# Retention attention and a noisy top-2 router on one core: a later place for the weight casts of four experts in the order model, and new priority offsets for the expert tiles

## The chip, the core and the metric

The kernel runs on one core of a Trainium2 chip, in one launch. The metric is the device time of one execution in microseconds (us). Each time given is the median of several executions, with the lowest and the highest beside it. The engines are PE (TensorE), DVE (VectorE), ACT (ScalarE), POOL (GpSimd) and SP (SyncE, which only issues transfers here); PEld is PE's loading of weights.

## The reference

The inputs are q, k and v of 8 batches, 8 heads, 576 positions and 64 channels, gate weights, noise, and two weight matrices for each of 8 experts (512 to 1024, and 1024 to 512).

```
scores = (1/8) * q @ k^T                               # per batch and head
Dmat   = gamma_h ** (i - j) where i >= j, else 0       # gamma_h = 1 - 2**(-5-h)
x      = ((scores * Dmat) @ v) as [4608 tokens, 512]   # heads side by side
logits = x @ w_gate + log1p(exp(x @ w_noise)) * noise
top2, weights = the 2 largest of 8 logits, softmax of the two
out[token] = sum over its 2 experts e: weight * (relu(x @ w1[e]) @ w2[e])
```

There is no softmax in the attention, so it is computed in chunks with carried states. Each token goes through two of the eight experts only.

## The kernel before

**How the work is staged.** The attention is done in 16 units of four heads of one batch. Four units and a `tail` (the last 64 positions) make one batch pair, and after each of the four pairs comes `route`: logits on PE (L967), the choice of two experts in some twenty small DVE operations (L977 to L1012, ending with the one-hot matrix MM at L1003), ranks by a triangular matmul on PE (L1030, L1032), a product on POOL (L1041), table positions on DVE, and then two large one-hot products on DVE: `olo` and `oh` (both L1074) and `oh` times values (L1076). PE multiplies these (L1081) into a table `xi` of the tokens of each expert (L1092 to L1099). PE also turns the attention's result into rows (L1110), which SP stores to a buffer `xd` in DRAM.

In one unit, POOL or DVE scales q and v (L721, L728), PE transposes k and q (L744, L750), ACT copies the transposes (L459), PE computes scores (L775), DVE masks them (L783, four per unit), PE makes the states (L808, copied by ACT) and the result (L843, L853). The `tail` has its own lines: products on POOL (L881, L884), transposes (L893), scores (L908), masks on DVE (L913), results (L926, L930).

**The experts.** Each expert has a fixed number of places for tokens, in tiles of 128 rows. Tiles whose tokens are known early run in gaps of the attention: 11 early tiles of one or two row blocks, i = 0 to 10, in the order of experts 0, 0, 1, 1, 2, 2, 0, 1, 2, 3, 3. POOL gathers the rows of a tile by indirect DMA (L1246, tiles `xg`), PE transposes them (L1268), ACT or DVE copies (L459, L461; the latter is DVE's form of the same copy), PE runs the first layer (`up`, L1328), ACT or DVE the relu (L1337, L1339), PE the second layer (`down`, L1418), ACT or DVE the weighting (L1471, L1473), and POOL scatters the rows to the output (L1483). After them come the `wide` tiles of up to four row blocks (first layer L1354, transposed by DMA), the second layer of each tile interleaved with the first of the next.

**The weights.** Experts 0 to 2 are loaded by casting DMAs that POOL issues (L1159, L1163). Expert 3 takes the place of the attention's `xT`, and experts 4 to 7 take the places of 0 to 3: for these, `part` lets SP load eight pieces in f32 (L1183, L1186) to `big` tiles, and ACT or DVE casts each to bf16 (L1188).

**What sets the order.** Nothing is reordered on the chip: each engine runs its own stream in order. The streams are written by a list scheduler, `Plan.run`. `Kernel.record` first enters all operations, each with a model cost, its reads and writes, a buffer class and a priority `prio`. `run` then again and again takes the ready operation with the smallest (earliest model start in steps of 0.05 us, `prio`, number of entry). An operation with two allowed engines goes to the one where the model ends it sooner. The earliest start takes in when an operand is there; for an operand that a DMA brings, `hold` us of the operation are added.

`Plan.op` adds to the given `prio` an offset from the table ORDER, by the name `at` of the operation and a bucket of the given `prio`: buckets 0 to 3 for 0 to 59, bucket 4 for 60 to 135, bucket 5 from 136 up. The attention and the routing lie in 0 to 3. An early tile i is entered at 100 + 4i: tiles 0 to 8, and the casts of expert 3 (60), lie in bucket 4, tiles 9 and 10 and all wide tiles in bucket 5. Offsets of one step of `prio` decide only between operations that the model could start at the same time. Two fillers follow from the model too: `warm` puts matmuls without use (L467) where the model sees PE idle in the first 170 us, and `rest` (L444) puts a memset between indirect DMAs.

Of the kernel before, what the change touches and what calls it, by code (L numbers as in the profile page):

```python
# [21 lines left out]
F = 1024  # L22
# [134 lines left out]
    "route48": (-0.5, -0.25, -1.5, 0, -0.5, -0.5),  # L157
    "route49": (2, 5, 0.5, -1.5, 2, 2),
    "route50": (-2.5, -2, -2, -6.5, -2.5, -2.5),
    "overflow_table1": (-2, -2, -2, -2, -2, -2),  # L160
    "overflow_table2": (-2, -2, -2, -2, -2, -2),
    "overflow_table3": (-0.25, -0.25, -0.25, -0.25, -0.25, -0.25),
    "overflow_table4": (-2, -2, -2, -2, -2, -2),
    "weights1": (-0.75, -0.75, -0.75, -0.75, -0.75, -0.75),
    "part1": (2, 2, 2, 2, 2, 2),
    "fetch1": (-5, -5, -5, -5, -6, -4),
    "fetch2": (-1.25, -1.25, -1.25, -1.25, -1.5, -2.25),
    "fetch3": (0.5, 0.5, 0.5, 0.5, -3, 1.5),
    "fetch4": (-0.25, -0.25, -0.25, -0.25, 0.75, 0.75),
    "fetch5": (0, 0, 0, 0, 0, -4),  # L170
    "fetch6": (-4, -4, -4, -4, -8.25, -1.5),
    "fetch7": (-1.25, -1.25, -1.25, -1.25, 6.5, -3.25),
    "fetch8": (-2.5, -2.5, -2.5, -2.5, -4, 0),
    "mix1": (0.25, 0.25, 0.25, 0.25, 0.25, 0.25),
    "mix2": (4, 4, 4, 4, 4, 4),
    "mix3": (2.25, 2.25, 2.25, 2.25, 2.25, 2.25),
    "up1": (2, 2, 2, 2, 2, 2),
    "wide1": (2.75, 2.75, 2.75, 2.75, 2.75, 2.75),
    "wide2": (1.25, 1.25, 1.25, 1.25, 1.25, 1.25),
    "finish1": (-2.25, -2.25, -2.25, -2.25, -2.25, -2.25),  # L180
    "finish2": (0, 0, 0, 0, 0, 5.5),
    "finish3": (5.75, 5.75, 5.75, 5.75, 24, 6.75),
    "finish4": (5.5, 5.5, 5.5, 5.5, 5.5, 5.5),
    "record1": (3, 3, 3, 3, 3, 3),
    "record2": (1.75, 1.75, 1.75, 1.75, 1.75, 1.75),
    "record3": (6.5, 6.5, 6.5, 6.5, 6.5, 6.5),
    "record4": (2, 2, 2, 2, 2, 2),
}
BIG = 1.0e6
NOV = NCOL * E  # L190
# [223 lines left out]
class Kernel:  # L414
    def __init__(self, tc, ctx, src, gates, noise, w1, w2, out, xd):
# [761 lines left out]
    def part(self, e, k, prio, after):  # L1177
        pl, nc = self.pl, self.nc
        w, t = self.W[e], pl.buf("big", "exp")

        def ld(_):
            if k < KD:
                nc.sync.dma_start(out=t.t, in_=self.w1[e, k * P:(k + 1) * P, :])  # L1183
            else:
                fo = 2 * (k - KD)
                nc.sync.dma_start(out=t.t.rearrange("p (fo d) -> p fo d", fo=2),  # L1186
                                  in_=self.w2[e, fo * P:(fo + 2) * P, :].rearrange("(fo fi) d -> fi fo d", fi=P))
        pl.op("SP", 0.55, ld, w=[t], prio=prio, dma=1.35, after=after)  # L1188
        pl.op({"ACT": 1.06, "DVE": 0.7}, 0, lambda g: self.copy(g, w.t[:, k * F:(k + 1) * F], t.t), hold=1,
              r=[t], w=[(w, k)], prio=prio, at="part1")  # L1190

    def tiles(self):
# [183 lines left out]
    def down(self, i, t):  # L1376
# [372 lines left out]
```

## Time and profile before

| | |
|---|---|
| median of 3 executions | 411.0 us (410.47 to 411.59) |
| profiled execution | 412.69 us |
| its span, first to last instruction | 411.1 us |
| granted PE clock, mean of the span | 0.989 |
| PE busy | 377.1 us, 92% |
| ACT, POOL, DVE busy | 272.3, 291.0, 148.2 us |
| bytes moved by DMA | 98.06 MB, mean 239 GB/s |

The time is that of one execution on the device; the span lies within it. A row of a timeline gives the start and the length of a run of like instructions in us, the engine, line and operation, output and inputs, the count, and in brackets how long the engine had been idle and what ended that ("issue" where the profile shows nothing that was waited for). The ends of matmuls are modelled, so PE's lengths overlap a little; starts are as recorded.

### The profile page before, as it was taken

To read this page: it belongs to the slowest core of one execution; us is meant where nothing else is said; L and a number is where in the kernel's file an instruction comes from. 1 tells how busy PE (TensorE), PEld (TensorE's weight loads), DVE (VectorE), ACT (ScalarE), POOL (GpSimd) and SP (SyncE) were. 2 spreads that over 40 slices of the span, in tenths; PEclk is the share of its full clock that TensorE was granted. 3 is DMA by queue.
4 is the path that set the end of the run, shared out by engine and by line. 5 is a ranking of instruction groups with operands and counts; after the bars stand their busy time and mean duration, and the time that the engine had idled before them with its cause. 6 is when DMAs were issued, how large, how long until landed. Compare 5 with 4: busy or idle time off the path is not lost.

```text
span 411.1 us, 11031 instructions
## 1 busy us (share of the span) xinstructions
PE 377.1 (92%) x4320; PEld 233.3 (57%) x4320; DVE 148.2 (36%) x413; ACT 272.3 (66%) x468; POOL 291.0 (71%) x379
## 2 busy tenths in 40 slices
PE   4998867889898898999999999999999999999994
PEld 2567656677575666767556554544554454454453
DVE  8456798788269587220111322101011000000002
ACT  2589978898787765776555877666686445555451
POOL 8676783990799848778676477778675776728564
PEclk9899999989999999999999999999999999999999
DMA  8999998999999989999989899999999998839766
GB/s 226 290 298 255 317 305 254 306 269 252 275 286 205 264 188 284 395 246 221 280 188 377 288 331 223 260 251 230 296 257 211 165 202 152 164 45 133 127 94 131
DMA packets 106184, 98.06 MB, mean 239 GB/s; under 512 B 40975, under 2 KB 83472, under 8 KB 106130
## 3 DMA queue, kind: packets, MB, share of 16 engines
q1 hardware_dynamic: 85858, 60.92, 56.0%
q0 software_dynamic: 17584, 36.24, 43.4%
q8 instruction: 34, 0.56, 0.6%
q10 hardware_dynamic: 2688, 0.18, 0.4%
q14 instruction: 20, 0.16, 0.2%
HBM read 73.11 MB, written 26.10 MB: 241 GB/s over the span
## 4 chain that ended last, share of the span: by engine, by line
PE 65%; DVE 8%; POOL 7%; DMA 6%; issue 6%; ACT 6%; POOLq 0%; SPq 0%; another core or an unknown queue 0%; DVEq 0%; ACTq 0%
PE ps L1418 25%; PE ps L1354 23%; PE ps L1328 6%; POOL out_dram L1483 4%; DMA xd<-xg 2%; ACT half L459 2%; DMA half<-in_v_dram 2%; DVE half L783 2%; PE ps L1437 2%; PE ps L808 2%; PE ps L467 1%; POOL half L721 1%; ACT xT L459 1%; DVE olo L1074 1%; PE ps L1268 1%
## 5 line engine op out<-in xcount | busy, mean ns | idle before, releaser
L1337 ACT ACTIVATE half<-ps 128x512 bf16<-128x512 f32 (+5 forms) x184 | 90.6, 503 | 87.5 <-PE ps L1354 55.0
L1418 PE MATMUL ps<-W,half 128*128 128x512 bf16 x432 | 137.8, 379 | 1.4 <-issue 1.1
L1354 PE MATMUL ps<-big,W 128*128 128x512 bf16 (+4 forms) x448 | 124.5, 326 | 0.6 <-DVE half L1473 0.6
L1246 POOL DMA_INDIRECT xg<-xd,xi x76 | 79.1, 1040 | 48.2 <-DMA half<-in_v_dram 11.7
L1483 POOL DMA_INDIRECT out_dram<-half,xg x71 | 90.3, 1272 | 30.1 <-issue 14.8
L1418 PEld LDWEIGHTS <-half 128*128 128x128 bf16 x568 | 54.5, 98 | 62.8 <-issue 3.1
L1354 PEld LDWEIGHTS <-W 128*128 128x128 bf16 x448 | 43.8, 98 | 33.4 <-issue 0.8
L1354 PE MATMUL ps<-big,xT 128*128 128x512 bf16 (+2 forms) x160 | 47.6, 337 | 0.0
L1471 ACT ACTIVATE half<-ps,xg 128x512 f32<-128x512 f32 (+1 forms) x58 | 39.3, 678 | 10.0 <-PE ps L1418 6.7
L783 DVE TENSOR_TENSOR half<-ps,mask 128x512 bf16<-128x512 f32 x64 | 40.3, 682 | 14.3 <-PE ps L775 10.9
L1418 PE MATMUL ps<-xT,half 128*128 128x512 bf16 x136 | 44.9, 379 | 0.0
L459 ACT ACTIVATE half<-ps 128x1024 bf16<-128x1024 bf16 (+1 forms) x42 | 38.5, 946 | 7.9 <-PE ps L744 4.0
L1473 DVE TENSOR_SCALAR half<-ps,xg 128x512 f32<-128x512 f32 (+1 forms) x17 | 10.6, 623 | 76.8 <-PE ps L1437 42.0
L1328 PE MATMUL ps<-half,W 128*128 128x256 bf16 (+1 forms) x288 | 29.1, 255 | 1.6 <-DVE half L461 0.8
L1339 DVE TENSOR_SCALAR half<-ps 128x512 bf16<-128x512 f32 (+5 forms) x12 | 6.8, 569 | 60.5 <-issue 32.9
L1328 PEld LDWEIGHTS <-W 128*128 128x128 bf16 x288 | 23.7, 98 | 5.8 <-issue 1.8
L467 PE MATMUL ps<-mask,ident__61 128*128 128x512 bf16 x68 | 20.3, 429 | 3.7 <-DVE hpf L527 3.7
L1469 DVE SCALAR_TENSOR_TENSOR half<-ps,xg,half 64x256 f32<-64x256 f32 (+2 forms) x7 | 3.6, 521 | 55.2 <-PE ps L1437 32.4
L1354 PEld LDWEIGHTS <-xT 128*128 128x128 bf16 x160 | 15.6, 98 | 12.8 <-issue 0.4
L459 ACT ACTIVATE tb<-ps 64x512 bf16<-64x512 f32 x32 | 18.9, 591 | 4.0 <-POOL half L721 1.9
L459 ACT ACTIVATE W<-big 128x1024 bf16<-128x1024 f32 x20 | 21.0, 1059 | 0.0
L808 PE MATMUL ps<-half,half 64*64 64x64 bf16 (+2 forms) x512 | 17.2, 213 | 1.7 <-ACT xT L459 1.6
(204 smaller groups left out, 517.0 us busy)
## 6 DMA issues: line engine op xcount, KB each, us to landing
big<-in_moe_w_dram SPq DMA_DIRECT2D x40, 512.0 KB
W<-in_moe_w_dram POOLq DMA_DIRECT2D x12, 512.0 KB
xd<-xg SPq DMA_DIRECT2D x16, 264.0 KB
W<-in_q_dram SPq DMA_DIRECT2D x16, 256.0 KB
big<-in_k_dram SPq DMA_DIRECT2D x8, 512.0 KB
big<-in_v_dram SPq DMA_DIRECT2D x8, 512.0 KB
big<-in_q_dram SPq DMA_DIRECT2D x16, 256.0 KB
W<-in_k_dram SPq DMA_DIRECT2D x6, 512.0 KB
```

The lines of the kernel that those rows point to most:

```text
L459: self.nc.scalar.activation(out, in_, Act.Copy)
L467: self.nc.tensor.matmul(b.t, lhsT=ident, rhs=mask.rearrange("p r x -> p (r x)").unsqueeze(1).to_broadcast([P, 2, 2 * P]), start=True, stop ...
L783: nc.vector.tensor_tensor(S.t.bitcast(BF16).rearrange("p (h c x) -> p h c x", h=2, c=2)[:, h], p[h].t.rearrange("p (c x) -> p c x", c=2), ...
L808: nc.tensor.matmul(o[h * HD:(h + 1) * HD, hp, n, :], lhsT=kk[:k, r, c, y], rhs=vv[:k, r, c, y].unsqueeze(1).to_broadcast([k, n.stop - n.st ...
L1246: ins = nc.gpsimd.indirect_dma_start(out=x.t[:n, :], out_offset=None, in_=self.xd[:rows, :], in_offset=IOff(ap=xi.t[:n, h:h + 1], axis=0), ...
L1328: nc.tensor.matmul(pv()[:, f2, :], lhsT=w.t[:, o:o + P], rhs=xv()[:, di, :n], start=(di == 0), stop=(di == KD - 1))
L1337: self.nc.scalar.activation(o, i, Act.Relu)
L1354: self.mm = nc.tensor.matmul(p.t[:, :n], lhsT=w.t[:, o:o + P], rhs=xv()[:, di, :n], start=(di == 0), stop=(di == KD - 1))
L1418: self.mm = self.nc.tensor.matmul(po.t, lhsT=hv[:, c:c + P], rhs=self.W[e].t[:, o:o + DM], start=(f == 0), stop=(f == KF - 1))
L1471: nc.scalar.activation(y.t[q, c], x, Act.Copy, scale=g()[q])
L1473: nc.vector.tensor_scalar(y.t[q, c], x, g()[q], None, Alu.mult)
L1483: ins = nc.gpsimd.indirect_dma_start(out=self.out[:, :], out_offset=IOff(ap=ix()[q2], axis=0), in_=y.t[q2, :], in_offset=None, bounds_chec ...
```

## The change

There are two edits. The first is in `part`: the model starts the cast of a piece of the experts above 3 no sooner than 6 us after its landing, not 1 us. The second gives 31 rows of ORDER, those for the work on expert tiles, new offsets in buckets 4 and 5; buckets 0 to 3 stay.

```diff
-    "part1": (2, 2, 2, 2, 2, 2),
+    "part1": (2, 2, 2, 2, 197.5, 100.25),
...
-    "fetch4": (-0.25, -0.25, -0.25, -0.25, 0.75, 0.75),
+    "fetch4": (-0.25, -0.25, -0.25, -0.25, -90.5, -66.25),
...
-    "up1": (2, 2, 2, 2, 2, 2),
+    "up1": (2, 2, 2, 2, -254.75, -8.5),
...
-    "record1": (3, 3, 3, 3, 3, 3),
+    "record1": (3, 3, 3, 3, -86.5, -152),
...
-        pl.op({"ACT": 1.06, "DVE": 0.7}, 0, lambda g: self.copy(g, w.t[:, k * F:(k + 1) * F], t.t), hold=1,
+        pl.op({"ACT": 1.06, "DVE": 0.7}, 0, lambda g: self.copy(g, w.t[:, k * F:(k + 1) * F], t.t), hold=6 if e > 3 else 1,
               r=[t], w=[(w, k)], prio=prio, at="part1")
```

With the early offsets an operation of an early tile sorts ahead of attention work (up1 are the relus, fetch4 the copies of the transposed rows, record1 the second layer), and the casts of expert 3 (part1) behind everything of the early tiles. The streams are the same up to about 89 us of the program before. From there on they differ in places, until the last tiles; the tiles come in the same order, and in the wide stage PE's stream has the same sequence. PE has four more fillers.

On DVE, in the routing of the third batch pair, the products were interleaved with the masks of the last attention unit (L783) and of the tail (L913). Before:

```order
L1074 TENSOR_TENSOR olo<-iota,ps_127 128x2304
L783 TENSOR_TENSOR half_94<-ps_125,mask 128x512
L783 TENSOR_TENSOR half_94<-ps_126,mask 128x512
L783 TENSOR_TENSOR half_91<-ps_128,mask 128x512
L783 TENSOR_TENSOR half_91<-ps_129,mask 128x512
L1074 TENSOR_TENSOR oh<-iota,ps_127 128x1440
L913 TENSOR_TENSOR half_84<-ps_126,maskt 128x256
L913 TENSOR_TENSOR half_84<-ps_130,maskt 128x256
L1076 TENSOR_TENSOR oh<-oh,ps_127 128x1440
L1092 TENSOR_SCALAR Ls<-ps_128 128x80
```

And now:

```order
L1074 TENSOR_TENSOR olo<-iota,ps_124 128x2304
L1074 TENSOR_TENSOR oh<-iota,ps_124 128x1440
L1076 TENSOR_TENSOR oh<-oh,ps_124 128x1440
L461 COPY xg_109<-ps_125 128x2x512
L913 TENSOR_TENSOR half_96<-ps_126,maskt 128x256
L913 TENSOR_TENSOR half_96<-ps_124,maskt 128x256
L1092 TENSOR_SCALAR Ls<-ps_130 128x80
L1094 TENSOR_TENSOR ps_130<-Ls,ps_130 128x80
L1095 TENSOR_TENSOR xi_188<-L,ps_130 128x40
```

The three products stand in one run, and the masks of the last attention unit come after the table. A little ahead of this, one L721 of that unit, on POOL before, stands on DVE.

On PE at the same place, the 32 matmuls of the first layer of expert 1's first tile (L1328) stood after the attention, 8 just ahead of the third L1081 and 24 ahead of the last L1030. Now all 32 stand ahead of the third L1081, in two runs of 16 with 16 L1110 between, right behind the transposes of the tile's rows; the last attention unit, from its L775 on, follows that L1081. This is what stood right ahead of the ranks of the last pair (L1030) before:

```order
L1328 MATMUL ps_130<-half_87,W_122 128x256
L1030 LDWEIGHTS ltri
L1030 MATMUL ps_128<-MM,ltri 128x2x72
L1032 LDWEIGHTS ones
L1032 MATMUL ps_128<-MM,ones 128x2x72
```

And what stands there now (W_122 holds the weights of expert 1):

```order
L1328 MATMUL ps_131<-half_83,W_122 128x128
L1030 LDWEIGHTS ltri
L1030 MATMUL ps_129<-MM,ltri 128x2x72
L1032 LDWEIGHTS ones
L1032 MATMUL ps_129<-MM,ones 128x2x72
```

The L1328 with 256 columns was the first tile of expert 1; the one with 128 columns is its second, so the 16 L1418 of the first tile and 24 of the 32 first-layer matmuls of the second have gone ahead of L1030.

On PE near the tail of the second pair, L893 stood behind 16 L1110 and 4 L1418; now it stands behind 10 L1418, and the L1110 follow it. On ACT near 88 us of the program before, the copy of the first early tile's transposed rows stands ahead of two copies of the attention, and on PE the first L1328 stands behind L843 and L853 of that unit, not ahead of them.

On POOL, the product L1041 of the last pair. Before (W_123 is expert 2, xg_119 and xg_120 the rows of its tiles):

```order
L1483 DMA out_dram<-half_89,xg_115 4608x512
L1163 DMA W_123<-in_moe_w_dram 128x4x512
L1041 TENSOR_TENSOR ub<-MM,bnd 128x144
L1246 DMA xg_119<-xd,xi_188 128x264
L444 MEMSET idle 128x256
```

And now:

```order
L1483 DMA out_dram<-half_90,xg_115 4608x512
L1163 DMA W_123<-in_moe_w_dram 128x4x512
L1246 DMA xg_119<-xd,xi_188 128x264
L444 MEMSET idle 128x256
L1246 DMA xg_119<-xd,xi_188 128x264
L1163 DMA W_123<-in_moe_w_dram 128x4x512
L1246 DMA xg_120<-xd,xi_188 128x264
L1041 TENSOR_TENSOR ub<-MM,bnd 128x144
L1246 DMA xg_120<-xd,xi_188 128x264
```

The two gathers of xg_119, the last weight piece of expert 2 and one gather of xg_120 have moved ahead of L1041. Three of expert 3's eight casts are on DVE now, where all eight were on ACT.

More of the change, by code (lines that the diff above doesn't have):

```diff
@@ L159 @@
     "route50": (-2.5, -2, -2, -6.5, -2.5, -2.5),
[L160 to L163, printed above, removed]
+    "overflow_table1": (-2, -2, -2, -2, 41.75, -10.25),
+    "overflow_table2": (-2, -2, -2, -2, 1.75, -63.25),
+    "overflow_table3": (-0.25, -0.25, -0.25, -0.25, 13, -10.75),
+    "overflow_table4": (-2, -2, -2, -2, -104, -32),
@@ L164 @@
     "weights1": (-0.75, -0.75, -0.75, -0.75, -0.75, -0.75),
-    "part1": (2, 2, 2, 2, 2, 2),
-    "fetch1": (-5, -5, -5, -5, -6, -4),
-    "fetch2": (-1.25, -1.25, -1.25, -1.25, -1.5, -2.25),
-    "fetch3": (0.5, 0.5, 0.5, 0.5, -3, 1.5),
-    "fetch4": (-0.25, -0.25, -0.25, -0.25, 0.75, 0.75),
[L170 to L174, printed above, removed]
@@ L175 @@
-    "mix2": (4, 4, 4, 4, 4, 4),
-    "mix3": (2.25, 2.25, 2.25, 2.25, 2.25, 2.25),
-    "up1": (2, 2, 2, 2, 2, 2),
[L178 to L183, printed above, removed]
-    "record1": (3, 3, 3, 3, 3, 3),
-    "record2": (1.75, 1.75, 1.75, 1.75, 1.75, 1.75),
@@ L186 @@
-    "record3": (6.5, 6.5, 6.5, 6.5, 6.5, 6.5),
-    "record4": (2, 2, 2, 2, 2, 2),
+    "part1": (2, 2, 2, 2, 197.5, 100.25),
+    "fetch1": (-5, -5, -5, -5, 2.25, -1.75),
+    "fetch2": (-1.25, -1.25, -1.25, -1.25, -86.5, -57.75),
+    "fetch3": (0.5, 0.5, 0.5, 0.5, -73.25, -107.5),
+    "fetch4": (-0.25, -0.25, -0.25, -0.25, -90.5, -66.25),
+    "fetch5": (0, 0, 0, 0, 69, 143.75),
+    "fetch6": (-4, -4, -4, -4, -65, 18.5),
+    "fetch7": (-1.25, -1.25, -1.25, -1.25, 40.25, -41.75),
+    "fetch8": (-2.5, -2.5, -2.5, -2.5, 6.75, -55.5),
@@ new lines @@
+    "mix1": (0.25, 0.25, 0.25, 0.25, -10, 29),
+    "mix2": (4, 4, 4, 4, -124.25, 18.5),
+    "mix3": (2.25, 2.25, 2.25, 2.25, -28, 18),
+    "up1": (2, 2, 2, 2, -254.75, -8.5),
+    "wide1": (2.75, 2.75, 2.75, 2.75, 21, 62.25),
+    "wide2": (1.25, 1.25, 1.25, 1.25, 16, -6),
+    "finish1": (-2.25, -2.25, -2.25, -2.25, -47, -24.5),
+    "finish2": (0, 0, 0, 0, -77, -4.75),
+    "finish3": (5.75, 5.75, 5.75, 5.75, 96.75, -164),
+    "finish4": (5.5, 5.5, 5.5, 5.5, 0.75, -57.75),
+    "record1": (3, 3, 3, 3, -86.5, -152),
@@ L188 @@
+    "record2": (1.75, 1.75, 1.75, 1.75, 26.5, 82.5),
+    "record3": (6.5, 6.5, 6.5, 6.5, -53, -145),
+    "record4": (2, 2, 2, 2, -83.75, -63.5),
 }
```

## The prediction

> **What bounds the kernel now.** I read the profile's page first, for the shares of the engines.
>
> ```profile
> span 411.1 us, 11031 instructions
> PE 377.1 (92%) x4320; PEld 233.3 (57%) x4320; DVE 148.2 (36%) x413; ACT 272.3 (66%) x468; POOL 291.0 (71%) x379
> ```
>
> PE carries the kernel, so time can be saved only where PE waits. The windows view cuts the span into stages: window and length, then the busy time of PE, PEld, DVE, ACT and POOL with counts, PE's granted clock, DMA share, GB/s.
>
> ```profile
> 101.60:130.00 28.40, 25.48 (x503) 18.73 (x503) 15.38 (x54) 23.05 (x39) 23.81 (x27) 1.00 1.07 260
> 130.00:149.00 19.00, 15.50 (x321) 11.68 (x320) 13.20 (x32) 13.67 (x25) 12.78 (x17) 1.00 1.12 260
> 149.00:161.00 12.00, 12.00 (x128) 8.82 (x126) 11.12 (x34) 7.84 (x16) 10.47 (x19) 1.00 0.83 177
> 161.00:195.00 34.00, 32.16 (x266) 21.59 (x265) 6.07 (x13) 21.90 (x34) 27.32 (x42) 1.00 1.04 297
> 206.00:406.00 200.00, 199.04 (x1176) 104.27 (x1174) 23.37 (x54) 120.59 (x215) 137.12 (x113) 1.00 0.98 208
> ```
>
> From 206 us to 406 us PE is idle for 0.96 us of 200. Experts 4 to 7 are all computed there, and the clock is 1.00, so what the change does to that stage can gain next to nothing. Whatever is gained must come from the stage in which the early tiles run between the attention: PE is idle 2.92 us in 101.6 to 130, 3.50 in 130 to 149, none in 149 to 161, 1.84 in 161 to 195. That is 8.3 us, the whole prize, if what follows simply starts earlier. The timeline of PE names these waits in brackets, with who ended each.
>
> ```profile
> 95.25 0.83 PE L1328 MATMUL ps<-half,W 128*128 128x256 bf16 x6 [0.57 <-DMA W<-in_moe_w_dram]
> 105.37 1.05 PE L1110 MATMUL ps<-ident__61,xT 128*128 128x128 bf16 x16
> 106.26 1.03 PE L1418 MATMUL ps<-W,half 128*128 128x512 bf16 x4
> 108.91 0.62 PE L893 MATMUL ps<-ident__61,half 128*128 128x128 bf16 x8 [1.62 <-POOL half L881]
> 132.75 0.24 PE L775 MATMUL ps<-half,half 64*64 64x128 bf16 x2 [0.81 <-ACT xT L459]
> 139.55 0.30 PE L843 MATMUL ps<-half,half 64*64 64x128 bf16 x6 [1.16 <-issue]
> 142.04 0.81 PE L1081 MATMUL ps<-oh,olo 128*128 128x80 f16 x18
> 148.61 0.22 PE L1030 MATMUL ps<-MM,ltri 128*128 128x144 bf16 x1 [0.46 <-DVE MM L1003]
> 149.24 3.62 PE L1418 MATMUL ps<-W,half 128*128 128x512 bf16 x16
> 152.69 1.95 PE L1328 MATMUL ps<-half,W 128*128 128x128 bf16 x32
> 163.59 1.69 PE L1418 MATMUL ps<-W,half 128*128 128x512 bf16 x7 [1.11 <-issue]
> 170.54 3.65 PE L1328 MATMUL ps<-half,W 128*128 128x256 bf16 x32 [0.37 <-DVE half L461]
> 174.03 0.61 PE L1268 MATMUL ps<-ident__61,xg 128*128 128x128 bf16 x8
> 189.86 3.65 PE L1328 MATMUL ps<-half,xT 128*128 128x256 bf16 x32
> ```
>
> A group's us include modelled ends, so I take prices from start to start: a 512-column L1418 costs (152.69 − 149.24) / 16 = 0.216 us, a 256-column L1328 (174.03 − 170.54) / 32 = 0.109, an L1110 (106.26 − 105.37) / 16 = 0.056. The reader should see that the waits are many and short, and that each sits where PE's stream had nothing that was ready to put there.
>
> **The hold of the casts.** Expert 4's casts end on ACT with the first of these rows, and the second is the first L1354 that reads them.
>
> ```profile
> 235.17 2.06 ACT L459 ACTIVATE W<-big 128x1024 bf16<-128x1024 f32 x2
> 268.57 0.38 PE L1354 MATMUL ps<-big,W 128*128 128x512 bf16 x1
> ```
>
> From 237.2 to 268.6 are some 31 us for the first of the four experts, and the stage has no PE wait to remove, so a cast put later by 5 us is still early. I cost the hold at 0, gain or loss. Its cover is that margin; if it were gone, the price would be one 128x1024 cast, 0.97 us (half of the pair at 87.91 below).
>
> **Early copy on ACT, and the fillers (about 90 us).** On ACT the copy of the first early tile's gathered rows now stands ahead of two copies that the attention waits for.
>
> ```profile
> 87.91 1.94 ACT L459 ACTIVATE half<-ps 128x1024 bf16<-128x1024 bf16 x2
> 90.04 0.65 PE L775 MATMUL ps<-half,half 64*64 64x128 bf16 x32
> ```
>
> L775 follows that pair, so it starts one copy later: +0.97 us. In return the first L1328 now stands behind L843 and L853, where the 0.57 us for its weights is covered: −0.57. Sum +0.4; ends 0 and +0.97. The four new fillers (L467, 512 columns) are 4 × 0.216 = 0.86 us, and lie in the 0.97 us in which PE waits for that copy; without the copy's delay they would cost 0.86. I take 0.
>
> **L893 (109 us).** Before, 16 L1110 (0.89 us) and 4 L1418 (0.86) fill the time to L893, which still waits 1.62 us. Now 10 L1418 fill it, 10 × 0.216 = 2.16, and the L1110 come after. −0.4; ends 0 and −0.41, since the releaser L881 stays at its place on POOL.
>
> **The routing of the third batch pair (124 to 149 us).** This is the largest term. The rows of DVE:
>
> ```profile
> 129.42 2.54 DVE L1074 TENSOR_TENSOR olo<-iota,ps 128x2304 f16<-128x2304 f16 x1
> 131.88 1.28 DVE L783 TENSOR_TENSOR half<-ps,mask 128x512 bf16<-128x512 f32 x2
> 134.94 1.64 DVE L1074 TENSOR_TENSOR oh<-iota,ps 128x1440 f16<-128x1440 f16 x1
> 138.53 1.64 DVE L1076 TENSOR_TENSOR oh<-oh,ps 128x1440 f16<-128x1440 f16 x1
> L721 DVE TENSOR_TENSOR half<-W,tabq x2: 1214/1218/1221, 8.8 to 18.4; 128x1024 bf16<-128x1024 f32 x2
> ```
>
> Now the two L1074 and L1076 stand back to back: 2.54 + 1.64 + 1.64 = 5.82 us. One L721, on POOL before, comes ahead of them on DVE with 1.22 us. So they end near 129.42 + 1.22 + 5.82 = 136.5 instead of 140.2, and L1081 can follow there, not at 142.04. The last attention unit, formerly interleaved with them, moves behind L1081. PE meanwhile has the first layer of expert 1's first tile, 32 L1328 or 3.5 us, with 16 L1110 between (0.9). PE's idle in 130 to 149 is 3.50 us. The 1.16 us of it inside a run of L843 is ended by no engine, so moving rows need not remove it: I keep it, and take 3.50 − 1.16 = 2.34 off. −2.3. The near end is 0: the moved unit now has its four L783 (two pairs of 1.28) in series with L843, and L1030 still needs the routing chain of the last pair, so the waits may return at those two. The far end is −3.5. What speaks for the middle is that 60 more matmuls stand ahead of L1030: 16 L1418, 24 narrow L1328 and 16 to 20 small ones, 3.45 + 24 × 0.056 (1.79 / 32 in the row at 152.69, whose successor starts at 154.48) + about 0.9 = 5.7 us of work that no longer stands behind L1030.
>
> ```profile
> 154.48 0.61 PE L1268 MATMUL ps<-ident__61,xg 128*128 128x128 bf16 x8
> 148.65 0.45 POOL L1041 TENSOR_TENSOR ub<-MM,bnd 128x144 f32<-128x144 bf16 x1 [4.38 <-DVE keep_w L1006]
> 162.93 0.60 ACT L1337 ACTIVATE half<-ps 128x512 bf16<-128x512 f32 x1 [2.64 <-remote]
> ```
>
> A rule of the Trainium skill speaks against the move of L721: by "SBUF — State Buffer", section "Who interferes with whom", a VectorE instruction with two SBUF inputs, as L721 has, and a GpSimd instruction that reads SBUF shut each other out for a whole instruction. The two L721 that ran on DVE here took 1.21 and 1.22 us, and no row shows one held up; by the rule up to one POOL product of about 1 us would come on top, an estimate from that page, and the term would be −1.3.
>
> **POOL's idle and the waits of 161 to 195 us.** On POOL, L1041 sat 4.38 us with gathers queued behind it. Now the gathers of expert 2's later tiles and its last weight piece go first. PE doesn't wait for these gathers before, so the idle is not itself PE time; the first wide gathers start some us earlier and nobody is late for them. What PE waits for in 161 to 195 is one L1418 held 1.11 us behind ACT's L1337 (162.93 + 0.60 = 163.53, PE goes on at 163.59), and 0.37 us. L1337's releaser isn't seen ("remote"), so I don't know that it goes: half of 1.11 + 0.37 is −0.7, plus nothing for the rest of that window. Ends 0 and −1.8 (the window's whole idle).
>
> **The sum.** +0.4 − 0.4 − 2.3 − 0.7 = −3.0 us. The profiled execution took 412.69 us, 1.59 around its span of 411.1, which I leave as it is; it gives 409.7. The median of the runs shown is 411.0, 1.7 below the profiled one, so the time is 411.0 − 3.0 = 408.0. The end is the same: the last 5 us are one scatter behind the last sum, in both.
>
> **The rivals.**
>
> *No change.* The early stage is a chain (attention unit, logits, router on DVE, one-hot products), and PE's waits only move to L1081, L843 and L1030. For it: L1030 waits for DVE already, 0.46. Against: the chain itself is cut, by 140.2 − 136.5. It gives 0.4 − 0.4 = 0, 411.0. Chance 0.20.
>
> *Slower: PE stops for expert 1's weights.* PE now meets expert 1's first L1328 not long after the third pair's L1030: by PE's stream 164 matmuls lie between. The load is issued where it was:
>
> ```profile
> 122.81 0.24 PE L1030 MATMUL ps<-MM,ltri 128*128 128x144 bf16 x1
> 122.59 1.54 POOL L1159 DMA_DIRECT2D W<-in_moe_w_dram x2
> 87.20 0.77 POOL L1159 DMA_DIRECT2D W<-in_moe_w_dram  x1
> ```
>
> Expert 0's second piece, issued at 87.20, let PE go on at 95.25, 8.05 us later. Expert 1's second piece is issued half of 1.54 us after 122.59, so by the same time it lands at 131.4. The 164 matmuls at the first window's mean, 25.48 / 503 = 0.051 us, bring PE there at 122.8 + 8.3 = 131.1: no margin at all. Behind the L1328 on PE stand L1110, L908 and L1081, so everything waits. Up to 131.1 + 3.0 = 134.1 it only eats the gain. With 14 us from issue to landing, three quarters longer, it lands at 137.4 and PE waits 6.3 us: 411.0 − 3.0 + 6.3 = 414.3. For it: the DMA share is over 1 in these windows. Against: 260 GB/s there, as in the window before. Chance 0.13, and 0.04 for a later landing or a wait of that size elsewhere.
>
> *A larger gain.* If the 8.3 us nearly all go, PE comes to expert 3's first layer (189.86) earlier, but that reads weights whose last cast on ACT starts so late:
>
> ```profile
> 181.80 1.06 ACT L459 ACTIVATE xT<-big 128x1024 bf16<-128x1024 f32 x1
> ```
>
> It ends at 182.86, so no more than 7.0 us can be passed on: 404.0. It takes every new place to be free of waits. Chance 0.08.
>
> **How the numbers follow.** The forecast has the rest, 0.55. A measurement tells about 0.3%, 1.2 us, from no change. Faster: 0.55 + 0.08 = 0.63; same: 0.20; slower: 0.17. The near ends of the terms sum to +0.97, 412.0; the far ends to −0.41 − 3.5 − 1.8 = −5.7, 405.3. The range takes in part of both outer rivals: 404.6 to 412.4; beyond it lie about 0.06 below and 0.14 above.
>
> **What would show it.** Right: POOL's L1041 without its 4.38 us; the L1074 and L1076 of the third routing in one run, L1081 near 137; L893's wait near 1.2; the last L1030 near 151 with expert 1's 16 L1418 ahead of it; the first wide L1354 some 3 us earlier; PE full after it, and the casts of experts 4 to 7 later with no one waiting. Wrong: a PE wait for a weight DMA at the first L1328 of expert 1 (near 131), waits over 1 us at L1081, L843 or L1030, or a new wait for a cast of expert 3.

## The result

| | before | after |
|---|---|---|
| median of 20 executions each, same chip | 410.9 us | 407.65 us |
| profiled execution | 412.69 us | 407.28 us |
| its span | 411.1 us | 405.7 us |
| ratio of times, 95% interval | 1 | 0.9922 [0.9899, 0.9944] |

The changed kernel is faster by 0.8%, or 3.2 us; 408.0 (404.6 to 412.4) had been forecast. The two profiled executions differ by 5.4 us, more than the medians, since the profile of before is 1.8 us above its median. Some executions of any of these kernels are disturbed and come out 1.5% or more above its fastest; the ratios leave them out, and the profiles of w1_first, pool_ahead and new_from_tile2 are of such executions, so only what lies ahead of the wide stage is read from them.

### The profile page after: what moved, and what is told of

Its sections match the earlier page's. It is cut to its first block, busy times and chain, and to the rows that moved or that the text cites. A ratio compares the mean times of both kernels' runs of the same rounds, so it can differ in the third digit from the quotient of the medians.

```text
span 405.7 us, 11025 instructions
## 1 busy us (share of the span) xinstructions
PE 375.5 (93%) x4324; PEld 234.7 (58%) x4324; DVE 148.2 (37%) x410; ACT 272.2 (67%) x472; POOL 289.1 (71%) x375
## 5 line engine op out<-in xcount | busy, mean ns | idle before, releaser
L1337 ACT ACTIVATE half<-ps 128x512 bf16<-128x512 f32 (+5 forms) x194 | 95.9, 500 | 76.8 <-PE ps L1354 57.9
L1418 PE MATMUL ps<-W,half 128*128 128x512 bf16 x432 | 137.7, 379 | 1.3 <-issue 1.3
L1354 PE MATMUL ps<-big,W 128*128 128x512 bf16 (+4 forms) x448 | 124.5, 326 | 0.0
L1246 POOL DMA_INDIRECT xg<-xd,xi x76 | 80.7, 1062 | 45.0 <-PE ps L1418 10.2
L1418 PEld LDWEIGHTS <-half 128*128 128x128 bf16 x568 | 54.7, 98 | 60.9 <-issue 1.8
L1354 PEld LDWEIGHTS <-W 128*128 128x128 bf16 x448 | 43.8, 98 | 33.2 <-issue 0.8
L1471 ACT ACTIVATE half<-ps,xg 128x512 f32<-128x512 f32 x59 | 40.4, 685 | 14.0 <-PE ps L1418 13.7
L1354 PE MATMUL ps<-big,xT 128*128 128x512 bf16 (+2 forms) x160 | 47.7, 337 | 0.0
L1473 DVE TENSOR_SCALAR half<-ps,xg 64x256 f32<-64x256 f32 (+1 forms) x16 | 9.3, 583 | 97.9 <-PE ps L1437 72.9
L1418 PE MATMUL ps<-xT,half 128*128 128x512 bf16 x136 | 44.7, 379 | 0.0
L783 DVE TENSOR_TENSOR half<-ps,mask 128x512 bf16<-128x512 f32 x64 | 40.1, 682 | 12.1 <-PE ps L775 9.1
L459 ACT ACTIVATE half<-ps 128x1024 bf16<-128x1024 bf16 (+1 forms) x43 | 39.4, 948 | 7.0 <-issue 3.1
L1328 PE MATMUL ps<-half,W 128*128 128x256 bf16 (+1 forms) x288 | 29.4, 255 | 1.7 <-DMA W<-in_moe_w_dram 1.4
L1328 PEld LDWEIGHTS <-W 128*128 128x128 bf16 x288 | 23.8, 98 | 5.1 <-DMA W<-in_moe_w_dram 1.7
L1354 PEld LDWEIGHTS <-xT 128*128 128x128 bf16 x160 | 15.6, 98 | 12.8 <-issue 0.4
L459 ACT ACTIVATE tb<-ps 64x512 bf16<-64x512 f32 x32 | 18.9, 590 | 6.2 <-PE ps L808 3.8
L459 ACT ACTIVATE W<-big 128x1024 bf16<-128x1024 f32 x17 | 17.9, 1052 | 4.3 <-DMA big<-in_moe_w_dram 4.3
L775 PE MATMUL ps<-half,half 64*64 64x128 bf16 x512 | 11.5, 217 | 8.4 <-ACT half L459 5.2
L721 POOL TENSOR_TENSOR half<-W,tabq 128x1024 bf16<-128x1024 f32 x6 | 11.4, 1902 | 10.0 <-DMA W<-in_q_dram 7.9
```

The lines of the kernel that those rows point to most:

```text
L459: self.nc.scalar.activation(out, in_, Act.Copy)
L721: self.eng(e).tensor_tensor(o, i, tabq.t[:, 2 * hq:2 * hq + 2].unsqueeze(3).to_broadcast([P, 2, 8, HD]), Alu.mult)
L775: nc.tensor.matmul(o[h][e * HD:(e + 1) * HD, c, r], lhsT=kt[s, hp, c, r, e, :], rhs=qt[s, hp, :, 16 * j:16 * j + 16], start=(c == 0 and r ...
L783: nc.vector.tensor_tensor(S.t.bitcast(BF16).rearrange("p (h c x) -> p h c x", h=2, c=2)[:, h], p[h].t.rearrange("p (c x) -> p c x", c=2), ...
L1246: ins = nc.gpsimd.indirect_dma_start(out=x.t[:n, :], out_offset=None, in_=self.xd[:rows, :], in_offset=IOff(ap=xi.t[:n, h:h + 1], axis=0), ...
L1328: nc.tensor.matmul(pv()[:, f2, :], lhsT=w.t[:, o:o + P], rhs=xv()[:, di, :n], start=(di == 0), stop=(di == KD - 1))
```

## The profile after

The page's first lines, and the windows of PE, PEld, DVE, ACT and POOL (busy us and counts, then PE's clock, DMA share and GB/s). The first three windows are those shown of before; the next two are cut at 191 us, since the first wide L1354 now comes at 194.5.

```profile
span 405.7 us, 11025 instructions
PE 375.5 (93%) x4324; PEld 234.7 (58%) x4324; DVE 148.2 (37%) x410; ACT 272.2 (67%) x472; POOL 289.1 (71%) x375
```

```profile
101.60:130.00 28.40, 27.03 (x531) 19.82 (x524) 18.27 (x60) 23.72 (x41) 23.95 (x28) 1.00 1.12 262
130.00:149.00 19.00, 16.28 (x335) 12.65 (x333) 12.06 (x22) 13.80 (x25) 14.29 (x17) 1.00 1.14 268
149.00:161.00 12.00, 11.40 (x110) 8.22 (x109) 11.11 (x39) 7.66 (x17) 7.89 (x16) 1.00 0.82 208
161.00:191.00 30.00, 29.78 (x266) 21.00 (x264) 8.48 (x21) 20.31 (x34) 25.47 (x38) 1.00 1.13 281
202.00:401.00 199.00, 198.22 (x1173) 103.94 (x1170) 20.61 (x48) 122.12 (x220) 137.97 (x113) 1.00 1.01 216
```

PE's idle in the four early windows is 1.37, 2.72, 0.60 and 0.22 us, 4.9 together, where before had 2.92, 3.50, 0 and 1.84, 8.3 together. The wide stage has 0.78 idle in 199 us: it was full and stays full. So 3.35 of the 4.49 us by which the first wide L1354 came earlier (199.02 to 194.53) are PE idle that is gone. The remaining 1.1 us lies ahead of these windows, or in time that this view counts as busy, which modelled matmul ends allow.

PE's timeline at the places of the prediction; in brackets the idle before a run and what ended it.

```profile
92.61 0.64 PE L775 MATMUL ps<-half,half 64*64 64x128 bf16 x32 [0.67 <-ACT half L459]
106.33 2.32 PE L1418 MATMUL ps<-W,half 128*128 128x512 bf16 x10
108.49 0.61 PE L893 MATMUL ps<-ident__61,half 128*128 128x128 bf16 x8
...
130.98 0.38 PE L1328 MATMUL ps<-half,W 128*128 128x256 bf16 x2
132.75 1.70 PE L1328 MATMUL ps<-half,W 128*128 128x256 bf16 x14 [1.39 <-DMA W<-in_moe_w_dram]
137.27 0.82 PE L1081 MATMUL ps<-oh,olo 128*128 128x80 f16 x18
138.41 0.64 PE L775 MATMUL ps<-half,half 64*64 64x128 bf16 x32
144.96 0.60 PE L1418 MATMUL ps<-W,half 128*128 128x512 bf16 x2 [1.33 <-issue]
151.93 0.24 PE L1030 MATMUL ps<-MM,ltri 128*128 128x144 bf16 x1 [0.60 <-DVE MM L1003]
158.47 3.62 PE L1418 MATMUL ps<-W,half 128*128 128x512 bf16 x16
167.96 3.66 PE L1328 MATMUL ps<-half,W 128*128 128x256 bf16 x32
194.53 0.92 PE L1354 MATMUL ps<-big,W 128*128 128x448 bf16 x4
```

L893 no longer waits. L1081 starts at 137.27, 4.8 us earlier than before, behind one new wait of 1.39 us for expert 1's weights. The run of 16 L1418 at 158.47 is expert 2's first second layer, the place that waited 1.11 us before; it has no wait now. Two more waits of before are gone: the L1328 at 167.96 doesn't wait for DVE's copy (0.37 us before, at 170.54), and the L775 of the last attention unit, at 138.41, doesn't wait for ACT's copies. Before it waited twice, 0.81 us at 132.75 and again here:

```profile
133.24 0.41 PE L775 MATMUL ps<-half,half 64*64 64x128 bf16 x14 [0.24 <-ACT xT L459]
```

DVE and POOL around the third routing:

```profile
122.22 1.23 DVE L721 TENSOR_TENSOR half<-big,tabq 128x1024 bf16<-128x1024 f32 x1
130.29 2.54 DVE L1074 TENSOR_TENSOR olo<-iota,ps 128x2304 f16<-128x2304 f16 x1
132.75 1.65 DVE L1074 TENSOR_TENSOR oh<-iota,ps 128x1440 f16<-128x1440 f16 x1
134.43 1.65 DVE L1076 TENSOR_TENSOR oh<-oh,ps 128x1440 f16<-128x1440 f16 x1
```

```profile
122.23 1.53 POOL L1159 DMA_DIRECT2D W<-in_moe_w_dram  x2
151.96 0.46 POOL L1041 TENSOR_TENSOR ub<-MM,bnd 128x144 f32<-128x144 bf16 x1 [4.34 <-DVE keep_w L1006]
```

The three products stand in one run and end at 136.08 (136.5 was worked out). L1041 on POOL, however, still waits 4.34 us, with less queued behind it but for as long.

## The experiments

The theory after the result: the hold does nothing; the gain comes from the order of the early tiles on PE and its neighbours, and lies ahead of the wide stage. Its rivals were one part alone: DVE's run of products, the transfers that moved ahead on POOL, the last weight piece, or the first two tiles' places. Each of the four sets ran on a chip of its own, beside the kernel before, whose medians there were 419.7, 416.5, 414.5 and 411.1 us, so ratios are compared and not times. offsets_only and w1_first rest on three executions each, the fewest here.

| kernel | ratio to before | interval | segment, us | of it at half clock, us |
|---|---|---|---|---|
| before, profiled | 1 | | 116.4 | 3.4 |
| after, profiled | 0.9922 | [0.9899, 0.9944] | 109.6 | 0 |
| hold6_only | 0.9977 | [0.9943, 1.0012] | 118.4 | 3.4 |
| offsets_only | 0.9821 | [0.9733, 0.9908] | 114.3 | 0 |
| b4_only | 0.9847 | [0.9785, 0.9909] | 114.6 | 0 |
| new_to_tile1 | 0.9954 | [0.9920, 0.9988] | 119.1 | 6.8 |
| after_again | 0.9875 | [0.9822, 0.9927] | 113.1 | 0 |
| w1_first | 0.9929 | [0.9868, 0.9990] | 114.0 | 3.4 |
| dve_run | 0.9982 | [0.9945, 1.0019] | 117.7 | 6.8 |
| pool_ahead | 1.0033 | [0.9991, 1.0076] | 116.3 | 6.8 |
| w2_ahead | 1.0033 | [0.9995, 1.0072] | 118.9 | 3.4 |
| gathers_ahead | 1.0032 | [0.9990, 1.0074] | 121.8 | 13.7 |
| w2_late | 0.9962 | [0.9908, 1.0016] | 112.8 | 0 |
| new_from_tile2 | 0.9983 | [0.9933, 1.0033] | 113.8 | 3.4 |

The segment is worked out in each profile from PE's starts: from the L1030 of the second batch pair (82.63 in before, 84.89 in after) to the first wide L1354. It holds the same work in all, but for the four fillers. PE's streams are the same up to that L1030, and yet it starts anywhere from 82.6 to 87.7 us in these executions, which is why the segment doesn't begin at zero.

The clock is the other reason for care. In every trace PE's granted clock is 1.0 but for the last few us and some stretches of 3.4 us, or twice that, in which it is 0.5. Where PE is full, such a stretch can cost half its length, 1.7 us: in before 32 L808 take 1.56 us from start to start at 85.02, and 0.95 us at 91.01. They lie at places that differ between the executions: in before one lies at 84.9 to 88.3 us, inside the segment, and in after one at 79.1 to 82.5, just ahead of it. The windows view shows them as a lower mean clock (the figure behind POOL's count), here of before and then of after:

```profile
80.00:100.00 20.00, 16.99 (x399) 13.93 (x398) 18.07 (x50) 17.69 (x28) 13.35 (x19) 0.91 1.13 264
80.00:90.00 10.00, 8.89 (x225) 7.68 (x222) 7.75 (x37) 8.78 (x15) 9.80 (x16) 0.87 1.07 282
```

Ahead of 101.6 us both have two such stretches, so the 4.49 us above aren't of the clock. Of before and the five kernels that keep its order of expert tiles, every profile has such a stretch inside the segment; of the six with the new order from tile 2 on, one has. Whether the order has a hand in that isn't shown. The segment of one profile doesn't tell the kernel's time either: new_to_tile1 has a longer one than before and a ratio under 1, new_from_tile2 a shorter one and a ratio near 1.

From the first wide L1354 to PE's last start it takes 205.4 us in after and 206.4 in before.

### Which of the two edits

hold6_only is before with the hold alone, offsets_only is after without it.

```diff
-        pl.op({"ACT": 1.06, "DVE": 0.7}, 0, lambda g: self.copy(g, w.t[:, k * F:(k + 1) * F], t.t), hold=1,
+        pl.op({"ACT": 1.06, "DVE": 0.7}, 0, lambda g: self.copy(g, w.t[:, k * F:(k + 1) * F], t.t), hold=6 if e > 3 else 1,
```

> The kernel before with the one edit of the hold (6 us for experts 4 to 7), no new offsets. The streams are those of before up to the casts of expert 4, about 230 us. Theory (the gain comes from the early stage, PE has no wait to lose after 206 us): ratio to before 1.000 within 0.003, 411 us, PE idle from 206 us on still near 1 us. Rival (in before, ACT or DVE stands at the head of its queue waiting for a cast's data, and PE pays for it): a ratio near 0.996 or lower.

> The changed kernel with the hold back at 1 us: the new offsets alone. Its streams are those of the changed kernel up to about 225 us. Theory: the offsets carry the whole gain, ratio 0.992 (0.989 to 0.995), about 407.7 us, first wide L1354 near 194.5 us as in the changed kernel. Rival (the hold has its share): 0.996.

The hold alone gives 0.9977 with 1 inside the interval, the offsets alone 0.9821, which is a larger gain than the 0.989 to 0.995 that was expected; its first wide L1354 comes at 199.4 us and not near 194.5. PE's idle from 206 to 400 us in the hold's profile is 1.32 us (0.65 in before), of which the waits view explains one:

```profile
PE ps L1354 <- ACT half L1337: 0.2, 1, 0.2
```

So no wide matmul is seen to wait for a cast that stands later, and the offsets carry the gain by themselves. A gain of up to 0.6% from the hold lies inside its interval and isn't excluded.

### Which bucket, and which tiles

b4_only has the new column 4 alone. new_to_tile1 has the new offsets for the first two early tiles alone (priorities 100 to 107), with the old column 4 as a seventh entry for the later tiles; new_from_tile2 is its complement. Both keep column 5 and the hold new.

```diff
-            prio += ORDER[at][min(3, int(max(0.0, prio)) // 4) if prio < 60 else 4 if prio < 136 else 5]
+            prio += ORDER[at][min(3, int(max(0.0, prio)) // 4) if prio < 60 else (-1 if prio >= 108 or prio < 100 else 4) if prio < 136 else 5]
```

> The kernel before with the new offsets of bucket 4 alone (early tiles 0 to 8 and the casts of expert 3), bucket 5 and the hold as before. Streams as in the changed kernel up to the last L1081, about 163 us. Theory: what is gained is gained in the early tiles, ratio 0.993 (0.990 to 0.996), about 408 us, and the first wide L1354 within 1 us of 194.5. Rival (bucket 5, the order around expert 3 and the wide tiles, carries a good part): 0.996 or more, first wide L1354 near 197.

> The changed kernel with the new offsets of bucket 4 only for the first two early tiles; tiles 2 to 8 and the casts of expert 3 have the old ones. Its PE stream is that of the changed kernel up to about 117 us (so the early copy and the earlier L1418 ahead of L893 are in), and behind it DVE's products of the third routing are interleaved with the masks of the last attention unit again, as before. Theory (the third routing's stretch and what follows it carry 3 of the 3 us): ratio 0.998 (0.995 to 1.001), about 410.2 us, L1081 of the third routing near 141 us. Rival (the start of the early tiles already carries it, the routing only reflects it): 0.993, about 408 us.

> The changed kernel, but with the offsets of before for the first two early tiles (priorities 100 to 107): the complement of new_to_tile1, which had 0.9954. If the two parts of the gain add up, this part has the rest: against new orders at 0.982 to 0.992 as a whole, 0.990 (0.985 to 0.994) here, about 4 us; expert 2's first L1418 runs without a wait behind L1337 (under 0.3 us, where the old orders showed 1 to 3), and from the second L1030 to the first wide L1354 it takes about 115 us, between the old order's 116 to 122 and the new one's 110 to 115. Rival: the new order only works as a whole, because the later tiles can only move up where the first two made room. Then 0.998 to 1.002, the wait stands, and the segment takes 117 us or more.

b4_only has 0.9847: bucket 4 is enough. This too is more than was expected (0.990 to 0.996), and its first wide L1354 comes at 198.0 us, not near 194.5. The first two tiles alone have 0.9954; the interval leaves out 1 and holds both the 0.998 of the theory and the 0.993 of the rival. The third L1081 comes at 140.80, near 141 as expected, but 16.0 us after the third L1030, where the six profiles with the old order have 18.2 to 21.7 and those with the new one 14.5 to 16.6. Expert 2's L1418 waits behind ACT's L1337 as under the old order:

```profile
165.55 0.60 ACT L1337 ACTIVATE half<-ps 128x512 bf16<-128x512 f32 x1 [3.18 <-remote]
167.08 0.60 ACT L1337 ACTIVATE half<-ps 128x512 bf16<-128x512 f32 x1 [0.93 <-remote]
```

```profile
166.21 0.61 PE L1418 MATMUL ps<-W,half 128*128 128x512 bf16 x2 [2.48 <-issue]
167.73 4.02 PE L1418 MATMUL ps<-W,half 128*128 128x512 bf16 x10 [0.92 <-issue]
```

The complement did in these two places what the theory said: the segment takes 113.8 us, and expert 2's first L1418 follow the L1081 with no wait. Its third L1081 is as late as under the old order, 21.3 us after the third L1030:

```profile
161.65 0.81 PE L1081 MATMUL ps<-oh,olo 128*128 128x80 f16 x18
162.29 3.62 PE L1418 MATMUL ps<-W,half 128*128 128x512 bf16 x16
```

Its ratio, 0.9983, misses the 0.985 to 0.994 that was expected and is the rival's number. The interval reaches from 0.9933 to 1.0033, so it isn't shown that the two parts add up, nor that each needs the other. The product of the two ratios, 0.9954 × 0.9983 = 0.9937, lies inside the interval of the whole, 0.9899 to 0.9944.

### Expert 1's weights

after_again is the changed kernel once more; w1_first is the same with expert 1's first two L1159 moved ahead of two gathers and two L728 on POOL. The order that the planner gives out is rearranged by a helper; this is its body here, and the kernels below have others.

```diff
-        self.log = [(t, o.on, o.fin, o.prio) for o, t in order]
+        order = rearranged(order)
...
+i = [nth(order, "weights1", k) for k in (4, 5)]
+p = [k for k, (o, t) in enumerate(order[:i[0]]) if o.on == "POOL"]
+to = p[-4]
+w = [order[k] for k in i]
+for k in reversed(i):
+    del order[k]
+order[to:to] = w
```

> The changed kernel once more, on the chip of the three that follow, as what w1_first is compared with. Every theory: a ratio to before of 0.982 to 0.994, and in its trace a PE wait of 0.5 to 2 us for the weight DMA at the first L1328 of expert 1.

> The changed kernel with one move on POOL: the two L1159 that load the first-layer weights of expert 1 stand two gathers and two L728 earlier, some 4.4 us; no other engine's stream changes. Theory (the 1.39 us that PE waits at the first L1328 of expert 1 for these weights is a price that the change pays): that wait is gone, L1081 of the third routing is about 1 us earlier, bounded by DVE's L1076, and the time is 1.0 to 1.3 us under that of the changed kernel, ratio to it 0.997. Rival (the wait is hidden, since L1081, L843 or L1030 would wait for DVE instead): the wait moves there, and the ratio to the changed kernel is 1.000.

The wait for expert 1's weights, 1.39 us in the first profile of after, is absent from the second one, although the code is the same; there PE's longest wait from 85 to 200 us is one inside L843. With the weights issued earlier it is absent as well, and the interval of 0.9929 overlaps that of 0.9875. The expectation of a standing wait was a miss, and whether the earlier issue is worth anything stays open.

### DVE's products in one run

dve_run is before with L1074 and L1076 of the third routing directly behind the first L1074 on DVE; PE's order is untouched.

```diff
+i = [nth(order, "route38", 4), nth(order, "route38", 5), nth(order, "route39", 2)]
+w = [order[k] for k in [nth(order, "route35", 2)] + i[1:] if k > i[0]]
+order = [x for x in order if x not in w]
+i = nth(order, "route38", 4)
+order[i + 1:i + 1] = w
```

> The kernel before with one move on DVE: L1074 and L1076 of the third routing stand directly behind the first L1074, ahead of the four L783 of the last attention unit, as in the changed kernel; PE's stream stays as before. Theory (the run on DVE pays only since PE has the first layer of expert 1 to do meanwhile): L783 comes 3.3 us later, L843 waits for it, PE gains nothing at L1081, and the time is 1 to 2 us over before, ratio 1.002 to 1.005. Rival (the shorter routing chain is itself the gain): 2 us under before, ratio 0.995.

DVE's timeline, then PE's:

```profile
134.01 1.65 DVE L1076 TENSOR_TENSOR oh<-oh,ps 128x1440 f16<-128x1440 f16 x1
135.58 2.48 DVE L783 TENSOR_TENSOR half<-ps,mask 128x512 bf16<-128x512 f32 x4
```

```profile
136.32 1.07 PE L843 MATMUL ps<-half,half 64*64 64x128 bf16 x32 [1.08 <-DVE half L783]
143.47 0.81 PE L1081 MATMUL ps<-oh,olo 128*128 128x80 f16 x18
```

The products end at 135.66, earlier than in after, but L1081 starts at 143.47, later than the 142.04 of before: it stands behind the attention unit on PE, and that unit now waits 1.08 us for the masks that stand behind the products. The ratio is 0.9982 with 1 inside: neither the loss that the theory expected (1.002 to 1.005) nor a clear gain. DVE's run by itself is not shown to gain anything. That it pays in after because L1081 stands there ahead of the unit, with other work to fill the time, fits both traces and was not tested apart.

### What moved ahead of L1041 on POOL

All three start from before. pool_ahead puts the two gathers of xg_119 and expert 2's last weight piece ahead of the last L1041, gathers_ahead the gathers alone, w2_ahead the weight piece alone. Their bodies differ in which operations are put ahead of L1041 (`route21`); this is that of w2_ahead:

```diff
+i = nth(order, "route21", 3)
+w = order.pop(nth(order, "weights1", -1))
+order.insert(i, w)
```

> The kernel before with one move on POOL: the two gathers of xg_119 and the last weight piece of expert 2 go ahead of the last L1041, in the 4.38 us in which POOL sat idle; no other stream changes. Theory (PE doesn't wait for what POOL does here): ratio 1.000 within 0.003, and PE still waits some 1 to 3 us at expert 2's first L1418 behind ACT's L1337 (near 164 us). Rival (this wait, seen in the three kernels with the old order of tiles 2 to 8, hangs on the lateness of POOL's transfers): it goes, and the ratio is 0.993 to 0.997.

> The kernel before with one move on POOL: the last weight piece of expert 2 (L1163) goes directly behind the piece before it, ahead of the last L1041, so it is issued some 8 us earlier; the gathers stay. Theory (the wait of 1.1 to 3.3 us at expert 2's first L1418, which the four kernels with the old order of tiles 2 to 8 show and the changed one doesn't, is a wait for this piece): the wait falls under 0.5 us, and the ratio to before is 0.994 to 0.998. Rival (it hangs on the gathers behind L1041, or on the order of PE and ACT): it stays, ratio 1.000.

> The kernel before with the other half of the same move: the two gathers of xg_119 go ahead of the last L1041, the weight piece stays behind it. Theory (the wait at expert 2's first L1418 is for the weight piece): it stays at 1 to 3 us, ratio 1.000 within 0.003. Rival (it is the gathers): it falls under 0.5 us, ratio 0.994 to 0.998.

The ratios are 1.0033, 1.0033 and 1.0032: none gains, and none is clearly slower. In w2_ahead the piece is issued at about 144, not 152.23, by POOL's timeline:

```profile
143.25 1.63 POOL L1163 DMA_DIRECT2D W<-in_moe_w_dram  x2
148.89 0.45 POOL L1041 TENSOR_TENSOR ub<-MM,bnd 128x144 f32<-128x144 bf16 x1 [4.01 <-DVE keep_w L1006]
```

The wait at expert 2's first second layer stands all the same in w2_ahead, on ACT and on PE:

```profile
164.67 0.60 ACT L1337 ACTIVATE half<-ps 128x512 bf16<-128x512 f32 x1 [1.72 <-remote]
```

```profile
165.32 2.33 PE L1418 MATMUL ps<-W,half 128*128 128x512 bf16 x10 [1.58 <-issue]
```

In gathers_ahead it is 1.75 us on ACT and 0.91 on PE. In pool_ahead, with both moved, it is all but absent, 0.18 us on PE, against what the theory expected, and the ratio is no better for it. So neither the weight piece alone nor the gathers alone remove the wait; for the two together there is one trace.

### The weight piece late again, in the new order

w2_late is after with that piece put back behind L1041 and one gather.

```diff
+i = nth(order, "weights1", -1)
+p = [k for k, (o, t) in enumerate(order) if k > i and o.on == "POOL"][:3]
+order.insert(p[-1], order.pop(i))
```

> The changed kernel with the last weight piece of expert 2 put back behind the last L1041 and a gather, some 8 us later, near where before had it relative to L1041. No other stream changes. Theory (the changed kernel owes the missing wait to the piece's earlier issue): PE waits 2 us or more at expert 2's first L1418, the first wide L1354 is later by about that, and the ratio to before goes from 0.988 to 0.992 or more. Rival (the new order of PE and ACT removed it): no wait there, and the ratio stays at 0.982 to 0.990.

The piece is issued at 156.96, 4.7 us later than in before, and expert 2's first second layer, which begins 4.8 us after that, has a wait of 0.20 us only:

```profile
156.96 0.82 POOL L1163 DMA_DIRECT2D W<-in_moe_w_dram  x1
```

```profile
161.75 1.03 PE L1418 MATMUL ps<-W,half 128*128 128x512 bf16 x4
162.98 2.75 PE L1418 MATMUL ps<-W,half 128*128 128x512 bf16 x12 [0.20 <-issue]
```

Its segment, 112.8 us, is that of the new order. So the wait at this place goes with the order, not with the time of the weight piece. The ratio points the other way: 0.9962 lies where the theory had it (0.992 or more), and its interval, from 0.9908 on, leaves out the rival's 0.982 to 0.990. If the late piece costs time, it does so by something other than this wait, and that is open.

## Why the prediction came out right, and where its steps were off

The verdict, the place (ahead of the wide stage) and the size (−3.0 forecast, −3.2 measured) hold. The terms hold less well, and that their sum came out so near is partly luck. This table cuts the segment at the L1030 of the third and fourth pair. "Profiled pair" is after less before. "Groups" is the mean of six profiles with the new order from tile 2 on (after, offsets_only, b4_only, after_again, w1_first, w2_late) less the mean of six with the old order (before, hold6_only, dve_run, pool_ahead, w2_ahead, gathers_ahead). The last column is the same, but takes for each stretch only the profiles in which it has no part at half clock: three, three and five of the old order, six, five and six of the new one. The changed kernels do 16 L1418, 24 narrow L1328 and some 14 L1268 more ahead of the fourth L1030, 16 × 0.216 + 38 × 0.056 = 5.6 us, which is taken off the second row and put on the third.

| stretch of PE's stream | forecast | profiled pair | groups | groups, full clock |
|---|---|---|---|---|
| second to third L1030 (copy, fillers, L893) | 0 | 37.03 − 40.18 = −3.15 | 38.35 − 39.76 = −1.4 | 38.35 − 39.07 = −0.7 |
| third to fourth (the third routing) | −2.3 | 30.01 − 5.6 − 25.80 = −1.4 | 30.10 − 5.6 − 26.11 = −1.6 | 30.06 − 5.6 − 25.31 = −0.9 |
| fourth L1030 to the first wide L1354 | −0.7 | 42.60 + 5.6 − 50.41 = −2.2 | 44.62 + 5.6 − 52.38 = −2.2 | 44.62 + 5.6 − 51.95 = −1.7 |

The four fillers, 0.86 us, lie in the first stretch, and sixteen L775, some 0.3 us, went from it into the second; neither is taken off.

- **Hold at 0**: not contradicted. hold6_only's interval holds it, with up to 0.6% of gain inside.
- **Early copy on ACT, +0.4, fillers 0**: the sum was +0.97 at L775 and −0.57 for the weights. L775's part was too large: over the groups its wait for the copy went from 0.23 to 0.66 us, +0.4. The wait of the first L1328 for its weights went from 0.59 us on the mean to 0 in all six, as forecast. Together that is −0.2 and not +0.4. That the fillers cost nothing was not tested apart.
- **L893, −0.4**: near it over the groups, though the profiled pair says otherwise. There the wait fell from 1.62 us to nothing. But it comes and goes: 1.6, 0.4, 0.5, 1.0, 0 and 0 us in the six profiles with the old order, 0, 0, 1.3, 0, 0.3 and 0 in the six with the new one, 0.58 and 0.27 on the mean, −0.3. Most of the pair's 1.62 belongs to one execution and not to the change.
- **The third routing, −2.3**: DVE's run and L1081 came as worked out (136.1 for 136.5, 137.3 for 137). The size was over-estimated: 0.9 to 1.6 us were passed on. The steadiest difference between the two orders lies here. L775's wait for ACT's copies (L459), 0.81 and 0.24 us in before, is 1.05 to 1.31 us in all six profiles with the old order and absent in all six with the new one. New waits took a part back. In the profiled execution 1.39 us went to PE's wait for expert 1's weights, which the prediction had named as a sign of being wrong. This is the slower rival's mechanism at the place it named: PE came to it at 130.98 (131.1 was forecast), and the weights came about 9.7 us after the middle of their issue (122.23 + 0.77 to 132.75), not 8.05. It was short of the 3 us at which it would have eaten the gain, and in the five other profiles with the new order it didn't appear at all.
- **The 1.16 us of "issue" inside L843, kept in the sum**: right in kind. A gap of 1.33 us is still there, now in front of two L1418 at 144.96. Two shorter gaps of the kind, 0.33 and 0.16 us in the same L843, were counted as gain.
- **POOL's idle**: wrong. L1041's 4.38 us were to go; 4.34 stayed. The fourth router itself (DVE's `keep_w`) came later, at about the same distance from POOL's work. The idle is not seen to be worth anything: with 0.97 us of it left in pool_ahead and 1.81 in gathers_ahead, the ratios are 1.003.
- **The waits of 161 to 195, −0.7**: mis-sized. Half of the wait at L1337 was taken, since its releaser was unknown. At expert 2's first second layer it went in full in five of the six profiles with the new order, and to 0.20 us in w2_late; on PE it had been 1.11, 3.25, 1.16, 1.58, 0.91 and 0.18 us in the six with the old order, 1.4 on the mean. The other half-taken wait, for DVE's copy (L461) ahead of L1328, 0.37 us in before and 0.8 on the mean, went in all six. Against that, in five of the six an L1418 waits 0.75 to 1.45 us further on, between 172 and 196 us; after alone has no such wait. PE's idle in this stretch fell from 3.4 to 1.9 us on the mean, and the stretch gave 1.7 to 2.2 us.
- **The rivals**: "no change" and "slower" didn't happen. The larger gain, capped at 404.0, is not reached by the median; the offsets alone and bucket 4 alone, 0.982 and 0.985, have intervals that overlap the whole change's 0.9875 on another chip, so no version is shown to beat it.

So the sum of −3.0 met the −3.2 of its chip with a routing term that was 0.7 to 1.4 us too large and a term for 161 to 195 that was 1.0 to 1.5 too small; the errors cancelled. The groups sum to −5.2 us, but 1.9 us of that go with the half clock; at full clock they sum to −3.3. Of the pair's −3.15 in the first stretch, up to 1.7 us are the half clock of before. The second chip's 0.9875 is −5.2 us of 416.5, with an interval that reaches to 0.9927, about −3.0, so nothing here says that −3.0 was too small.

What stays open is the cause of the wait at L1337, 1.7 to 3.3 us in five of the six profiles with the old order and in new_to_tile1. Its releaser can be narrowed down. In the five, the held L1337 waits for one semaphore, which in every trace PE's instructions alone raise, so it waits for PE's own first layer (L1328) and not for a DMA. "Remote" only says that the signal fits no recorded end of a PE instruction. In before the signal came at 162.91, 2.0 us after the start of the L1328 that raises it (160.91); elsewhere it comes some 0.3 us after it (157.64 to 157.93). Why it came so late was not shown. gathers_ahead and w2_late have much the same transfers ahead of L1041 and the weight piece behind it; the first, with the old order, waits, and the second, with the new one, does not. So at this place the wait goes with the order of the tiles from the third on. But b4_only, after_again and w1_first have an L1337 that is held in the same way, 0.9 to 1.6 us, at 191 to 193 us. Only after and new_from_tile2 have neither such an L1337 nor, between the fourth L1030 and the wide stage, an L1418 that waits with no releaser shown. They are also the only two traces in which nearly all of PE's signals on this semaphore are recorded (516 of 516 and 507 of 511; 449 to 472 of 511 to 523 in the others). That a part of these waits goes with the execution, or with its recording, is a rival that no run settles.

## What to carry to other kernels

When an order changes in many places, cost each wait whole, with its releaser's distance from the work ahead of it, and expect small sums of small terms: of a prize of 8.3 us of idle, some 3.4 was taken. Compare groups of profiles: a wait of 1.6 us in one execution was 0 in the next of the same order. Look at the clock of each stretch first: 1.9 us of a difference of 5.2 between two groups went with stretches at half clock. A move on one engine alone (DVE's run, POOL's transfers, a weight piece) showed no gain here; the gain came with an order in which PE's own stream was changed too. An engine's long idle in front of a product, such as POOL's 4.4 us, is no prize until a row shows who waits for it.

## What the hardware showed that was not expected

PE stops where no engine releases it, at places that go by the number of the instruction and not by the work. In before it stopped 1.16 us at 139.55, inside a run of L843; in after 1.33 us at 144.96, between L1418. Counted along PE's stream, weight loads and the sequencer's rows taken in, these are rows 5058 and 5314, 256 apart. hold6_only, where some rows are missing, stops at both places, 1.29 us at 137.76 and 0.73 at 144.06. The page of after lists the queue that carries instructions:

```profile
q8 instruction: 34, 0.56, 0.6%
```

0.56 MB in 34 packets is 16 KB each, or 256 rows of 64 bytes. In the trace a packet of this queue begins at 137.20 in before and at 142.64 in after, lasts 0.88 us, and PE goes on 1.4 to 1.5 us after its end (139.55 and 144.96). The other traces agree: in the ten that hold all matmuls, PE stops 54 times for over 0.3 us with no releaser, and 29 of these stops, of 0.35 to 3.8 us, stand at one of two neighbouring rows of a block of 256, each 1.3 to 1.7 us after the end of such a packet. This suggests that PE ran short of instructions there; no run changed only that. The Trainium skill, "Runtime: NRT & Kernel Launch", section "Instruction fetch mechanics", tells of a refill in blocks of 16 KiB whose cost is mostly hidden; the block's size agrees, and in before and after up to 1.3 us were not hidden, in stretches of many short matmuls at a DMA share of 1.1.
